# A fused attention and two-layer feed-forward kernel: attention's loads issued by ScalarE, the weight sums' stores by GpSimd, a second set of sums in the first pair

## The chip, the cores and the metric

One core of a Trainium2 chip. The metric is the device time of one execution, in microseconds. DVE is VectorE, ACT is ScalarE, POOL is GpSimd, SP is SyncE; PE is TensorE.

## The reference

Three functions in a chain, all in float32, over 4 batches of 768 tokens (3,072 in all) with 8 heads of 64.

```python
for c in range(S // 32):                      # chunks of 32 queries
    k_full = concat(mem_k, k[l_start:r_end])  # 8 memory keys; 16 to the left, 8 to the right
    a = softmax(q_c @ k_full.T / 8)
    out[chunk] = a @ v_full
x  = out as tokens x 512
xn = x / sqrt(mean(x * x) + 1e-6) * rms_g
h1 = (silu(xn @ w_gate) * (xn @ w_val)) @ w_out            # 512 -> 1536 -> 512
h  = h1 @ w_in
g  = where(h >= 1, h, where(h <= -1, 0, (h + 1)**2 / 4))
y  = g @ w_out2                                            # 512 -> 2048 -> 512
```

## The kernel before

**Arithmetic.** Every matrix product of the feed-forward layers is made of three products of high and low parts (lines 578 to 580 and 902 to 904): an operand is split into `hi`, rounded by ScalarE, and `lo`, the difference, made by DVE or GpSimd. The weights arrive as 64-bit words and are joined to float32 from the two halves of a word (`conv_c`, `join`).

**Tiles and stages.** The tokens are six tiles of 512 (TT). Tiles 0 to 3 (NS = 4) go one by one through the first layer: 12 blocks `f` of 128 features, three slots each, so 36 slots to a tile. Tiles 4 and 5 form a *pair* that is worked with seven products in place of eight (`seven`), on sums and differences of quarters of the inputs and of the weights. After it three pairs go through the second layer in the same way. Up to about 46 us the start is laid out engine by engine; tile 0 lasts to about 152 us, tiles 1 to 3 to about 269, 380 and 490 us, the first pair to about 640 us.

**What sets the order.** From tile 1 on every engine's order is the order in which the program writes its instructions. Each slot of a tile is a fixed place for background work, and `slot()` runs in it, in this order: what the slot before left in `later`, the attention step of that slot, one step of `xq` (if it has any), `conv_step`, and what stands in `after`.

**Attention beside the tiles.** A *unit* is four heads of 256 tokens; `pr` counts pairs of two units. `att_slot` with the table `plan2` spreads a pair over 11 slots: scores `s0` and `s1` in slots 0 and 3, transposes `a0`, `a1` in 2 and 5, values `v0`, `v1` in 4 and 7, normalization `r0` in 9, and transposes of the finished rows `x0`, `x1` in 10 and 12. Right after a unit's scores `att_step` loads k_in (two) and q_in of the next unit (`load_qk`, lines 391 and 392), after its values v_in (`load_v`). Line 425 is the scores, 450 the exponentials, 455 the transposes of them, 471 the values, 511 the squares, 530 the reciprocal root rs on GpSimd, 538 and 541 the scaling of x_nat, 551 its transposes, 567 their copies with rms_g (g_t), and 569 the stores of the finished x into DRAM (x_d) for tiles 2 and later.

**Sums of weights.** In tiles 1 to 3 a list of small steps (`steps`, taken by `conv_step`) prepares what the pairs need. `sum_steps` builds the first layer's sums, `w2_steps` and `pair_sums` the second layer's. A set of sums is two tiles S: DVE writes them (`sums`, lines 192 to 196), ScalarE rounds them (`hi_s`, 199), DVE takes the difference (`lo_s`, 202), and both parts are stored to DRAM (w1p_d, w1o_d, w2p_d, w2o_d; line 204). The quarters that need no sum go to DRAM as they are (`raws`, lines 239 and 243, "w1p_d<-wall"; for the second layer line 297). `load_w2` (line 270) loads the second layer's words into a ring of three tiles. The last of these steps run in the first pair, where S is the one tile `m2["late"]`.

**Preparing the pair.** In tile 3 both tiles' x come back as y from x_d (line 800), and `x_steps` makes the seven combinations from it in 12 steps, one per slot: the first is DVE's line 842, the rounding is ACT's 832, the differences are DVE's 835. `proj_in` and line 867 and 879 are the first layer's own gate and product, 593 and 595 the split of the hidden tile h into hh and hl. In the pair `seven` keeps three products per block in a ring `t` (`tmp2`; lines 922, 929, 933, 949, 954, 955).

Which queue carries what, before: SP the attention loads, x_d, the sums' stores, and all weight loads of the pairs; GpSimd the raws and the second layer's words.

Of the kernel before, what the change touches and what calls it, by code (L numbers as in the profile page):

```python
# [8 lines left out]
F32 = mybir.dt.float32  # L9
F32R = mybir.dt.float32r  # L10
BF16 = mybir.dt.bfloat16
U32 = mybir.dt.uint32
# [4 lines left out]
P = 128  # L17
# [14 lines left out]
TT = 512  # L32
# [8 lines left out]
def tile_stream_attention_moe_moe2(  # L41
# [10 lines left out]
    nc = tc.nc  # L52
    NT, DM = out.shape
    F1 = wts1.shape[0] // 3
    F2 = wts2.shape[0] // 2
    KK = DM // P
# [4 lines left out]
    pool = lambda name, bufs, **kw: ctx.enter_context(tc.tile_pool(name=name, bufs=bufs, **kw))  # L61
# [8 lines left out]
    moe1_only = ctx.enter_context(ExitStack())  # L70
    pool1 = lambda name, bufs: moe1_only.enter_context(tc.tile_pool(name=name, bufs=bufs))
    const1 = pool1("const1", 1)
    small = pool1("small", 2)
    wst = pool1("wst", 3)
    tmp = pool1("tmp", 3)
    single_only = moe1_only.enter_context(ExitStack())
# [3 lines left out]
    wall2 = poolS("wall2", 1).tile([P, 15, 2, 512], F32R, name="wall2")  # L80
    sp = poolS("sp", 3)
    sums_ = poolS("sums", 1)

    half = const.tile([P, 1], F32, name="half")

# [1 line left out]
    ident = const.tile([P, P], F32, name="ident")  # L87
    wall = wpool.tile([P, 21, 2, 512], F32R, name="wall")
    g_b = const1.tile([P, DM], F32, name="g_b")
    nhalf = const1.tile([P, 2], F32, name="nhalf")  # L90
    g_t = const1.tile([P, KK], F32, name="g_t")

    def unit(i):
        if i < 14:
# [14 lines left out]
    NS = NTT - 2  # L109
# [91 lines left out]
    def lo_s(S, k, h, dst):  # L201
        tt_(out=flat(S[k]), in0=flat(S[k]), in1=h.bitcast(F32), op=ALU.subtract)
        for n, src in enumerate((h.bitcast(F32), flat(S[k]))):
            nc.sync.dma_start(dst(n, k), src.rearrange("p (k c) -> p k c", k=2))

    def in_dst(dp):
        return lambda n, k: dp[:, 3 + 2 * k:5 + 2 * k, n]
# [6 lines left out]
    def at(n, fn):  # L214
        while len(steps) <= n:
            steps.append([])
        steps[n].append(fn)
# [4 lines left out]
    def sum_steps(i, srcs, raws, order, dst):  # L222
        n = 8 * i
        h, S = [], []

        def whole():
            if i % 2:
                h.extend(tmp.tile([P, 512], U32, tag="tu", name="wgv") for _ in range(2))
            else:
                gv = wst.tile([P, 1024], U32, tag="w64", name="wgv")  # L230
                h.extend([gv[:, :512], gv[:, 512:]])
            for x, w in zip(h, srcs):
                tt_(out=x.bitcast(F32), in0=w[:, 0], in1=w[:, 1], op=ALU.add)

        def first():
            S.extend(halves(wst.tile([P, 1024], F32, tag="w64", name="s1234")))
            sums(S, *order(h), True)

        at(n, lambda: (nc.gpsimd.dma_start(*raws[0]), whole()))
        at(n + 1, first)  # L240
        at(n + 2, lambda: sums(S, *order(h), False))
        for k, r in enumerate(raws[1:]):
            at(n + 2 + 2 * k, lambda r=r: nc.gpsimd.dma_start(*r))
        at(n + 4, lambda: hi_s(S, 0, h[0]))
        at(n + 5, lambda: hi_s(S, 1, h[1]))
        at(n + 6, lambda: lo_s(S, 0, h[0], dst))
        at(n + 7, lambda: lo_s(S, 1, h[1], dst))
# [18 lines left out]
    def load_w2(j):  # L266
        if j < 2 * F2:
            g, k = divmod(j, 4)
            w2raw[j] = wst.tile([P, 1024], U32, tag="w64", name="w64")
            nc.gpsimd.dma_start(w2raw[j], wts2[4 * g + (0, 2, 1, 3)[k]].bitcast(U32))  # L270

    W2 = 12 * F1 + 4

    def w2_steps(g):

        dp, do, u = w2p_d[g], w2o_d[g // 2], g % 2
        f32_ = {}

        part = lambda j, n: w2raw[j][:, 512 * n:512 * n + 512]

        def c(j):
            f32_[j] = g_b.bitcast(U32) if j % 4 == 3 else tmp.tile([P, 512], U32, tag="tu", name="tu")
            nc.scalar.activation(f32_[j].bitcast(F32), words(w2raw[j])[1].bitcast(F32), AF.Prelu, scale=2.0 ** -112, alpha=2.0 ** 32)

        def hi(j, n0, n1):
            nc.scalar.activation(part(j, 0)[:, n0:n1].bitcast(F32R), f32_[j].bitcast(F32)[:, n0:n1], AF.Copy)

        def lo(j, n0, n1, dsts):
            tt_(
                out=part(j, 1)[:, n0:n1].bitcast(F32),  # L290
                in0=f32_[j].bitcast(F32)[:, n0:n1],
                in1=part(j, 0)[:, n0:n1].bitcast(F32),
                op=ALU.subtract,
            )
            src = w2raw[j].bitcast(F32).rearrange("p (h c) -> p h c", h=2)
            for dst, c0, c1 in dsts:
                nc.gpsimd.dma_start(dst, src[:, :, c0:c1])

        dsts = [
            [(dp[:, 0], 0, 256), (dp[:, 1], 256, 512)],  # L300
            [(dp[:, 2], 256, 512)],
            [(do[:, 0, u], 0, 256)],
            [(do[:, 3, u], 0, 256), (do[:, 6, u], 256, 512)],
        ]
        for k in range(4):
            j, n = 4 * g + k, W2 + 28 * g + 7 * k
            n0, n1 = ((0, 512), (256, 512), (0, 256), (0, 512))[k]
            at(n, lambda j=j: c(j))
            at(n + 2, lambda j=j: join(f32_[j], w2raw[j]))
            at(n + 4, lambda j=j, n0=n0, n1=n1: hi(j, n0, n1))  # L310
            at(n + 6, lambda j=j, n0=n0, n1=n1, k=k: lo(j, n0, n1, dsts[k]))
            at(n + 13, lambda j=j: load_w2(j + 3))
        def pair_sums(a, b, n, order, dst):
            S, h = [], lambda: (f32_[a], f32_[b])

            def first():
                if m2["single"]:
                    S.extend([sp.tile([P, TT], F32, tag="s", name="s12"), sums_.tile([P, TT], F32, tag="s34", name="s34")])
                else:
                    S.extend(m2["late"][:, i] for i in range(2))  # L320
                S[:] = [x.rearrange("p (k c) -> p k c", k=2) for x in S]
                live.append(a)
                sums(S, *order(h()), True)

            at(n + 10, first)
            at(n + 11, lambda: sums(S, *order(h()), False))
            at(n + 13, lambda: hi_s(S, 0, f32_[a]))
            at(n + 14, lambda: hi_s(S, 1, f32_[b]))
            at(n + 15, lambda: lo_s(S, 0, f32_[a], dst))
            at(n + 16, lambda: (lo_s(S, 1, f32_[b], dst), live.remove(a)))  # L330

        pair_sums(4 * g, 4 * g + 1, W2 + 28 * g, rows_order, in_dst(dp))
        pair_sums(4 * g + 2, 4 * g + 3, W2 + 28 * g + 14, cols_order, out_dst(do, u))
# [44 lines left out]

    tails = []

    def load_qk(u):
        if u >= NU:
            return
        if u in (1, 2):
            kt = [hp_.tile([P, TT], F32, tag=t, name="k_in") for t in ("hh", "hl")]
            qt = sp.tile([P, TT], F32, tag="s", name="q_in")
        else:
            kt = [att.tile([P, TT], F32, tag=f"k{hp}", name="k_in") for hp in range(2)]
            qt = att.tile([P, 2 * PT], F32, tag="q", name="q_in")
        for hp in range(2):  # L390
            nc.sync.dma_start(kt[hp], k[u][:, hp * 512:hp * 512 + 512])
        nc.sync.dma_start(qt, q[u])
        qk_t[u] = (kt, qt)

    def load_v(u):
        if u >= NU:
            return
        n = 8 * (D + 1)
        if u < 4:
            if not tails:  # L400
                tails.append(xs.tile([P, 4, 2, D + 1], F32, tag="xn", name="v_tail"))
            tail = tails[0][:, u]
            nc.sync.dma_start(tail, v[u].rearrange("p (h c) -> p h c", h=2)[:, :, n - D - 1:])
            vt = [xs.tile([P, TT], F32, tag=f"x{'hl'[hp]}{u}", name="v_in") for hp in range(2)]
            m = n - D - 1
        else:
            vt = [att.tile([P, n], F32, tag=f"v{hp}", name="v_in") for hp in range(2)]
            m = n
        for hp in range(2):
            nc.sync.dma_start(vt[hp][:, :m], v[u][:, hp * n:hp * n + m])  # L410
        v_t[u] = [
            [tail[:, hp] if c == 7 and u < 4 else vt[hp][:, c * 65:c * 65 + 65] for c in range(8)]
            for hp in range(2)
        ]
# [139 lines left out]
    def part_X(pr, blk):  # L554
# [11 lines left out]
            for kk in range(KK):  # L566
                nc.scalar.activation(xn[:, kk], rows[:, kk], AF.Copy, scale=g_t[:, kk:kk + 1])
        if t >= 2:
            nc.sync.dma_start(x_d[t][:, :, c0:c0 + P], xn)

    def load_x(t):
        xn_t[t] = xs.tile([P, KK, TT], F32, tag="xn", name="xn")
# [158 lines left out]
    def att_step(pr, st):  # L731
# [8 lines left out]
        else:  # L740
            u = 2 * pr + n
            fns[st[0]](u, ps_a)
            for p in parts[st[0]]:
# [2 lines left out]
                    fn()  # L746
                else:
                    (later if p in "kp" else after).append(fn)
        if st[0] == "s":
            load_qk(2 * pr + n + 1)  # L750
        if st[0] == "v":
            load_v(2 * pr + n + 1)

    xq, after, later = [], [], []

# [39 lines left out]
    wo = {}  # L795
# [59 lines left out]
    for t in range(NS):  # L855
# [3 lines left out]
        for f in range(F1):  # L859
# [5 lines left out]
            proj_in(ps_g[0], w1[("g", f)])  # L865
            s = sp.tile([P, TT], F32, tag="s", name="s")
            nc.scalar.activation(s, ps_g[0], AF.Silu)
            slot(t, 3 * f)
            if t == NS - 1 and f == 6:
                att_only.close()  # L870
                right = ctx.enter_context(tc.tile_pool(name="right", bufs=1, side="right", reuse_waits="tile"))
                m2["y"] = right.tile([P, 2, KK, TT], F32, name="y")
                load_y(x_d[NS], x_d[NS + 1])
            if t == NS - 1 and f == 7:
                xq.extend(x_steps())
            proj_in(ps_g[1], w1[("v", f)])
            if f == F1 - 1 and t + 1 < NS:
                split_x(xn_t.pop(t + 1))
# [257 lines left out]
            m2[part] = parts[part]()  # L1136
        m2["n"] = 0

    second_pool(F1 // 2, 5, 6, "ring t wo h")
    m2["late"] = m2["pool"].tile([P, 2, TT], F32, name="s1234")  # L1140
    pair_bank.close()
    bpool = ctx.enter_context(
        tc.tile_pool(name="bpool", bufs=1, space=bass.MemoryType.PSUM, side="right", reuse_waits="tile")
# [135 lines left out]
```

## Time and profile before

| | |
|---|---|
| median of 3 runs | 1171.7 us (1169.03 to 1171.91) |
| the profiled execution | 1173.91 us |
| its span in the trace | 1172.1 us |
| mean granted TensorE clock | 0.987 of full speed |
| busy: TensorE, DVE, ScalarE, GpSimd | 97%, 70%, 53%, 10% of the span |
| moved by DMA | 281.81 MB, 240 GB/s over the span |

The span begins at the first instruction and ends with the last; times in the rows are microseconds from its start. "Busy" counts instructions in execution; issuing a DMA is shown in the rows under the issuing engine's queue (SPq, ACTq, POOLq) or engine, but is not counted. An instruction starts when its engine has come to it in program order and everything that it waits for has come: what ended its wait last stands in brackets behind it.

### The profile page before, as it was taken

What the parts mean: (1) busy time and instruction counts of PE and PEld (TensorE: products, weight loads), DVE (VectorE), ACT (ScalarE), POOL (GpSimd) and SP (SyncE); (2) the same over time, 40 slices, a digit from 0 to 9 for tenths busy, and PEclk for the clock granted to TensorE, in tenths of its full rate; (3) what the DMA queues carried; (4) which work ended last, traced back from release to release, by engine and by line L of the source; (5) the groups of instructions that cost most, each with busy time, mean ns of one, the idle gap of its engine ahead of it and who ended that gap; (6) DMA issues with size and microseconds to landing.
All of it is one profiled execution on the core that took longest, in us unless ns stands there. A gap on an engine that the chain in (4) does not pass through costs nothing.

```text
span 1172.1 us, 21039 instructions
## 1 busy us (share of the span) xinstructions
PE 1131.2 (97%) x7909; PEld 915.6 (78%) x7909; DVE 821.4 (70%) x1426; ACT 619.0 (53%) x1096; POOL 114.9 (10%) x165
## 2 busy tenths in 40 slices
PE   7889999999999999899989999999999999999998
PEld 5677787788787778788768888778887788887886
DVE  4777767677656676656647877897767887578855
ACT  4676655467665675434433734456434465444543
POOL 2500003122212123101110000000000000000000
PEclk7899999999999999999999999999999999999999
DMA  9765538798988797779998687766778666773564
GB/s 311 235 228 193 181 135 286 249 345 294 302 250 303 228 312 225 261 276 335 400 346 261 203 284 244 256 179 195 230 210 260 180 191 212 219 202 95 151 194 159
DMA packets 144212, 281.81 MB, mean 240 GB/s; under 512 B 15216, under 2 KB 65392, under 8 KB 142320
## 3 DMA queue, kind: packets, MB, share of 16 engines
q1 hardware_dynamic: 123664, 228.57, 60.9%
q0 software_dynamic: 12768, 43.52, 11.1%
q10 hardware_dynamic: 7680, 8.39, 2.0%
q8 instruction: 62, 1.02, 0.3%
q14 instruction: 38, 0.31, 0.1%
HBM read 201.26 MB, written 79.17 MB: 239 GB/s over the span
## 4 chain that ended last, share of the span: by engine, by line
PE 74%; DMA 9%; DVE 8%; ACT 5%; issue 2%; SPq 1%; POOL 1%; ACTq 0%; DVEq 0%; POOLq 0%
PE ps_y L1064 14%; PE ps_g L1064 10%; PE ps_g L578 5%; PE ps_g L580 5%; PE ps_g L579 5%; DMA w<-in_w_dram 3%; PE ps_g L902 3%; PE ps_b L902 3%; PE ps_b L904 3%; PE ps_b L903 3%; PE ps_g L904 3%; PE ps_g L903 3%; PE ps_y L578 3%; PE ps_y L579 2%; PE ps_y L580 2%
## 5 line engine op out<-in xcount | busy, mean ns | idle before, releaser
L1064 PE MATMUL ps_y<-r,wo 128*128 128x512 f32 x672 | 156.2, 390 | 0.0
L578 PE MATMUL ps_g<-xh,wall 128*128 128x512 f32 x384 | 156.1, 406 | 0.0
L580 PE MATMUL ps_g<-xh,wall 128*128 128x512 f32 x384 | 150.4, 392 | 0.0
L579 PE MATMUL ps_g<-xl,wall 128*128 128x512 f32 x384 | 150.3, 391 | 0.0
L1064 PEld LDWEIGHTS ps_y<-r,wo 128*128 128x128 f32 x672 | 125.7, 188 | 26.0
L1014 DVE TENSOR_TENSOR r<-h,r 128x512 fp32r<-128x512 f32 x167 | 112.0, 687 | 44.4 <-ACT r L1012 44.4
L965 ACT ACTIVATE t<-t,half 128x512 f32<-128x512 f32 x96 | 66.9, 720 | 128.4 <-DVE t L964 122.7
L1012 ACT ACTIVATE r<-h 128x512 fp32r<-128x512 f32 x167 | 100.7, 625 | 56.5 <-DVE r L1014 17.5
L1064 PE MATMUL ps_g<-r,wo 128*128 128x512 f32 x498 | 116.0, 390 | 0.0
L1064 PEld LDWEIGHTS ps_g<-r,wo 128*128 128x128 f32 x498 | 93.2, 188 | 19.4
L580 PEld LDWEIGHTS ps_g<-xh,wall 128*128 128x128 f32 x384 | 72.4, 188 | 15.9
L578 PEld LDWEIGHTS ps_g<-xh,wall 128*128 128x128 f32 x384 | 72.6, 189 | 15.6 <-issue 0.2
L902 PE MATMUL ps_b<-wall 128*128 128x512 f32 x202 | 79.9, 396 | 4.3 <-DVE t L933 4.0
L579 PEld LDWEIGHTS ps_g<-xl,wall 128*128 128x128 f32 x384 | 72.7, 189 | 13.5
L902 PE MATMUL ps_g<-wall 128*128 128x512 f32 x198 | 78.8, 398 | 4.3 <-DVE t L933 2.4
L904 PE MATMUL ps_b<-wall 128*128 128x512 f32 x202 | 79.2, 392 | 0.0
L903 PE MATMUL ps_b<-wall 128*128 128x512 f32 x202 | 79.2, 392 | 0.0
L579 PE MATMUL ps_y<-hl,wall 128*128 128x512 f32 x192 | 75.8, 395 | 3.0 <-DVE hl L595 3.0
L578 PE MATMUL ps_y<-hh,wall 128*128 128x512 f32 x192 | 78.1, 407 | 0.0
L903 PE MATMUL ps_g<-wall 128*128 128x512 f32 x198 | 77.3, 390 | 0.0
L904 PE MATMUL ps_g<-wall 128*128 128x512 f32 x198 | 77.2, 390 | 0.0
L580 PE MATMUL ps_y<-hh,wall 128*128 128x512 f32 x192 | 75.5, 393 | 0.0
(191 smaller groups left out, 2112.1 us busy)
## 6 DMA issues: line engine op xcount, KB each, us to landing
wo<-w2o_d SPq DMA_DIRECT2D x88, 512.0 KB, 3.6
wall<-w2p_d SPq DMA_DIRECT2D x168, 256.0 KB, 3.0
wall<-w1p_d SPq DMA_DIRECT2D x84, 256.0 KB, 5.7
w<-in_w_dram SPq DMA_DIRECT2D x36, 512.0 KB, 4.9
w<-in_w_dram POOLq DMA_DIRECT2D x32, 512.0 KB, 5.7
k_in<-in_k_dram SPq DMA_DIRECT2D x48, 256.0 KB, 4.7
wo<-w1o_d SPq DMA_DIRECT2D x21, 512.0 KB, 3.6
v_in<-in_v_dram SPq DMA_DIRECT2D x40, 260.0 KB, 4.4
```

The source lines that it names most:

```text
L578: nc.tensor.matmul(ps, wh, xh, start=start, stop=False)
L579: nc.tensor.matmul(ps, wh, xl, start=False, stop=False)
L580: nc.tensor.matmul(ps, wl, xh, start=False, stop=stop)
L902: nc.tensor.matmul(bank, wh, xh, start=st, stop=False, skip_group_check=True)
L903: nc.tensor.matmul(bank, wh, xl, start=False, stop=False, skip_group_check=True)
L904: nc.tensor.matmul(bank, wl, xh, start=False, stop=kk == 1, skip_group_check=True)
L965: nc.scalar.activation(s, s, AF.Square, scale=0.5, bias=half)
L1012: nc.scalar.activation(r[:, 0], src, AF.Copy)
L1014: tt_(out=r[:, 1], in0=src, in1=r[:, 0].bitcast(F32), op=ALU.subtract)
L1064: nc.tensor.matmul(bank[p][m], a, b, start=s0, stop=s1, skip_group_check=True)
```

## The change

Attention's loads for pairs 4 and later and the x_d stores are issued by ScalarE; the loads stand first in `after`, ahead of the exponentials or squares. The sums' stores (`lo_s`) go onto GpSimd's queue; the raws and `load_w2` go to SP. The first pair has two sets of sums and takes them in turn; the ring `t` has five tiles in place of six. `x_steps` begins with slot 24 (before it) in place of slot 22. The statistics tiles (ss, rs), nhalf and g_t are allocated last among the pools of the single tiles.

```diff
-    small = pool1("small", 2)
...
     sums_ = poolS("sums", 1)
+    small1 = poolS("small1", 1)
+    small = poolS("small", 2)
...
-    nhalf = const1.tile([P, 2], F32, name="nhalf")
-    g_t = const1.tile([P, KK], F32, name="g_t")
+    nhalf = small1.tile([P, 2], F32, name="nhalf")
+    g_t = small1.tile([P, KK], F32, name="g_t")
...
     def lo_s(S, k, h, dst):
...
-            nc.sync.dma_start(dst(n, k), src.rearrange("p (k c) -> p k c", k=2))
+            nc.gpsimd.dma_start(dst(n, k), src.rearrange("p (k c) -> p k c", k=2))
...
-        at(n, lambda: (nc.gpsimd.dma_start(*raws[0]), whole()))
+        at(n, lambda: (nc.sync.dma_start(*raws[0]), whole()))
...
-            at(n + 2 + 2 * k, lambda r=r: nc.gpsimd.dma_start(*r))
+            at(n + 2 + 2 * k, lambda r=r: nc.sync.dma_start(*r))
...
     def load_w2(j):
...
-            nc.gpsimd.dma_start(w2raw[j], wts2[4 * g + (0, 2, 1, 3)[k]].bitcast(U32))
+            nc.sync.dma_start(w2raw[j], wts2[4 * g + (0, 2, 1, 3)[k]].bitcast(U32))
...
-                    S.extend(m2["late"][:, i] for i in range(2))
+                    S.extend(m2["late"][a // 2 % 2][:, i] for i in range(2))
...
-    def load_qk(u):
+    def load_qk(u, eng=nc.sync):
...
-    def load_v(u):
+    def load_v(u, eng=nc.sync):
...
         if t >= 2:
-            nc.sync.dma_start(x_d[t][:, :, c0:c0 + P], xn)
+            nc.scalar.dma_start(x_d[t][:, :, c0:c0 + P], xn)
...
-        if st[0] == "s":
-            load_qk(2 * pr + n + 1)
-        if st[0] == "v":
-            load_v(2 * pr + n + 1)
+        if st[0] in "sv":
+            load = load_qk if st[0] == "s" else load_v
+            if pr < 4:
+                load(2 * pr + n + 1)
+            else:
+                after.insert(0, lambda: load(2 * pr + n + 1, nc.scalar))
...
+            if t == NS - 1 and f == 8:
+                xq.extend(x_steps())
             slot(t, 3 * f)
...
-            if t == NS - 1 and f == 7:
-                xq.extend(x_steps())
...
-    second_pool(F1 // 2, 5, 6, "ring t wo h")
-    m2["late"] = m2["pool"].tile([P, 2, TT], F32, name="s1234")
+    second_pool(F1 // 2, 5, 5, "ring t wo h")
+    m2["late"] = [m2["pool"].tile([P, 2, TT], F32, name=f"late{i}") for i in range(2)]
```

The line numbers of the changed kernel are one to three higher. The change moves instructions at three places that matter below. First SP's queue before, in tile 1, at a unit's scores; x_d is the store of finished rows, w1p_d the stores of sums (s_2317 their low parts, wgv the rounded ones):

```order
L569 DMA x_d_116<-x_nat 512x1x128
L204 DMA w1p_d_134<-wgv 128x2x256
L204 DMA w1p_d_134<-s_2317 128x2x256
L204 DMA w1p_d_134<-wgv 128x2x256
L204 DMA w1p_d_134<-s_2317 128x2x256
L391 DMA k_in<-in_k_dram 128x512 x2
L392 DMA q_in<-in_q_dram 128x512
L569 DMA x_d_116<-x_nat 512x1x128
```

The same place on ScalarE with the change:

```order
L594 ACTIVATE hh<-s 128x512
L568 ACTIVATE x_nat<-ps_a,g_t 128x128 x4
L570 DMA x_d_119<-x_nat 512x1x128
L392 DMA k_in<-in_k_dram 128x512 x2
L393 DMA q_in<-in_q_dram 128x512
L451 ACT_TABLE_LOAD
L451 ACTIVATE e<-e 128x512
L870 ACT_TABLE_LOAD
```

The loads stand between the copies of x_nat and the table load of the exponentials now, and the x_d stores have come along. Second, GpSimd before, in tile 2, where rs is made (w_... are the second layer's words):

```order
L270 DMA w_4495<-in_w_dram 128x1024
L297 DMA w2p_d_121<-w_4276 128x2x256 x2
L270 DMA w_4581<-in_w_dram 128x1024
L297 DMA w2p_d_121<-w_4391 128x2x256
L530 TENSOR_TENSOR rs<-ss,nhalf 128x2
L270 DMA w_4637<-in_w_dram 128x1024
L297 DMA w2o_d_128<-w_4495 128x2x256
```

and with the change:

```order
L205 DMA w2o_d_131<-s_4332 128x2x256
L205 DMA w2o_d_131<-g_b 128x2x256
L205 DMA w2o_d_131<-s_4333 128x2x256
L298 DMA w2p_d_124<-w_4273 128x2x256 x2
L298 DMA w2p_d_124<-w_4388 128x2x256
L531 TENSOR_TENSOR rs<-ss,nhalf 128x2
L205 DMA w2p_d_124<-tu 128x2x256
```

The word loads have gone; in their place the sums' stores (line 205) stand around rs. Third, VectorE before, in tile 3, where the inputs of the pair begin (line 842, y):

```order
L879 TENSOR_TENSOR s<-s,ps_g_109 128x512
L842 TENSOR_TENSOR y<-y 128x1024
L142 TENSOR_SCALAR tu<-tu 128x512
L143 SCALAR_TENSOR_TENSOR tu<-w_5619,tu 128x512
L202 TENSOR_TENSOR s_5652<-s_5652,tu 128x512
L595 TENSOR_TENSOR hl<-s,hh 128x512
L289 TENSOR_TENSOR w_5619<-tu,w_5619 128x256
L835 TENSOR_TENSOR wall<-y,wall 128x2x512
```

and with the change:

```order
L882 TENSOR_TENSOR s<-s,ps_g_112 128x512
L143 TENSOR_SCALAR tu<-tu 128x512
L144 SCALAR_TENSOR_TENSOR tu<-w_5622,tu 128x512
L203 TENSOR_TENSOR s_5655<-s_5655,tu 128x512
L596 TENSOR_TENSOR hl<-s,hh 128x512
L290 TENSOR_TENSOR w_5622<-tu,w_5622 128x256
L845 TENSOR_TENSOR y<-y 128x1024
L882 TENSOR_TENSOR s<-s,ps_g_112 128x512
```

y begins two slots later: the rest of its block's work, with the split of h (hl), comes first now, and y stands five rows further down, ahead of the next block's product.

## Rows read from the trace of the kernel before

**Rows 1.** The page, busy shares: busy us, share of the span, instructions.
```profile
PE 1131.2 (97%) x7909; PEld 915.6 (78%) x7909; DVE 821.4 (70%) x1426; ACT 619.0 (53%) x1096; POOL 114.9 (10%) x165
```

**Rows 2.** TensorE's waits: what waited <- for what; us in total, times, longest.
```profile
PE ps_s L551 <- DVE x_nat L541: 5.3, 1, 5.3
PE ps_a L425 <- DMA q_in<-in_q_dram: 4.1, 4, 2.9
PE ps_b L902 <- DVE t L933: 4.0, 1, 4.0
...
PE ps_y L579 <- DVE hl L595: 3.0, 1, 3.0
PE ps_g L902 <- DVE t L933: 2.4, 1, 2.4
...
PE ps_a L551 <- ACT x_nat L538: 1.7, 1, 1.7
```

**Rows 3.** Windows: us, busy us (instructions) of each engine, granted clock, DMA share, GB/s.
```profile
206.26:209.67 3.41, 3.41 (x70) 2.76 (x71) 2.11 (x4) 0.68 (x1) 0.00 (x0) 0.51 1.05 345
...
602.21:605.62 3.41, 3.35 (x8) 2.70 (x9) 0.72 (x3) 1.64 (x4) 0.71 (x1) 0.51 1.04 393
```

**Rows 4.** Timeline of SP's queue: start us, us, engine, line, operation.
```profile
193.13 0.65 SPq L204 DMA_DIRECT2D w1p_d<-wgv  x1
...
196.44 2.75 SPq L391 DMA_DIRECT2D k_in<-in_k_dram  x2
```

**Rows 5.** Chain that ended last, its DMA pieces: start us, us, what.
```profile
199.24 6.84 DMA q_in<-in_q_dram
...
570.45 7.34 DMA w2p_d<-s
...
591.73 8.65 DMA w2o_d<-s
```

**Rows 6.** Timeline of ScalarE: in brackets idle us before, and what ended it.
```profile
195.53 0.63 ACT L450 ACTIVATE e<-e 128x512 f32<-128x512 f32 x1 [1.76 <-DVE e L441]
```

**Rows 7.** Timeline of GpSimd (POOL).
```profile
375.84 0.55 POOL L270 DMA_DIRECT2D w<-in_w_dram  x1 [8.12 <-DMA w2p_d<-w]
```

**Rows 8.** Timeline at the start, GpSimd and VectorE.
```profile
31.49 1.45 POOL L243 DMA_DIRECT2D w1p_d<-wall  x2
...
33.71 4.24 DVE L541 SCALAR_TENSOR_TENSOR x_nat<-x_nat,rs,g_b 128x512 f32<-128x512 f32 x2 [1.82 <-POOL rs L530]
```

**Rows 9.** Timeline, TensorE and ScalarE, around the scores of a unit in tile 3.
```profile
420.89 0.86 PE L425 MATMUL ps_a<-k_in,q_in 64*32 64x64 f32 x64
...
424.83 1.28 ACT L450 ACT_TABLE_LOAD   x1
426.12 0.64 ACT L450 ACTIVATE e<-e 128x512 f32<-128x512 f32 x1
...
427.84 0.66 PE L455 MATMUL ps_a<-ident,e 128*128 128x128 f32 x4
...
431.18 0.86 PE L425 MATMUL ps_a<-k_in,q_in 64*32 64x64 f32 x64
```

**Rows 10.** Timeline of VectorE.
```profile
476.26 1.23 DVE L842 TENSOR_TENSOR y<-y 128x1024 f32<-128x1024 f32 x1 [7.14 <-DMA y<-x_d]
```

**Rows 11.** Timeline of VectorE in the first pair.
```profile
599.09 0.43 DVE L192 TENSOR_TENSOR s<-tu 128x256 f32<-128x256 f32 x1 [3.95 <-DMA w2o_d<-s]
```

**Rows 12.** DMA issues: count, KB, median us to landing; line 391: ns min/median/max.
```profile
w1p_d<-wall POOLq DMA_DIRECT2D x36, 256.0 KB, 5.0
...
q_in<-in_q_dram SPq DMA_DIRECT2D x24, 256.0 KB, 5.3
...
w1p_d<-s SPq DMA_DIRECT2D x24, 256.0 KB, 5.1
...
L391 SPq DMA_DIRECT2D k_in<-in_k_dram x48: 327/415/1574, 0.7 to 421.9; - x48
```

**Rows 13.** Windows, columns as in rows 3.
```profile
380.00:490.00 110.00, 106.91 (x958) 85.89 (x957) 72.14 (x142) 67.61 (x132) 24.94 (x37) 0.98 0.77 253
```

More of the change, by code (lines that the diff above doesn't have):

```diff
@@ L390, in load_qk @@
         for hp in range(2):
-            nc.sync.dma_start(kt[hp], k[u][:, hp * 512:hp * 512 + 512])
-        nc.sync.dma_start(qt, q[u])
+            eng.dma_start(kt[hp], k[u][:, hp * 512:hp * 512 + 512])
+        eng.dma_start(qt, q[u])
         qk_t[u] = (kt, qt)
-    def load_v(u):
+    def load_v(u, eng=nc.sync):
         if u >= NU:
@@ L409, in load_v @@
         for hp in range(2):
-            nc.sync.dma_start(vt[hp][:, :m], v[u][:, hp * n:hp * n + m])
+            eng.dma_start(vt[hp][:, :m], v[u][:, hp * n:hp * n + m])
         v_t[u] = [
```

## Prediction

> **What bounds the kernel now.** I read the page's busy shares first: TensorE is busy 97% of the span [rows 1]. No other engine can set the end by its mere amount of work, so the change is worth what TensorE's own waits are worth. The second view, TensorE's waits by what ended them, names these: 5.3 us once for the first normalized tokens, 2.9 us (the longest of four that make 4.1) for attention's q_in, 4.0 and 2.4 us for DVE's t at line 933, 3.0 us for hl, 1.7 us for x_nat behind ScalarE [rows 2]. Each wait is then followed back to the queue or buffer behind it, and that is where the parts of the change lie. The third view is the granted clock: after the waits of 2.9, 3.0 and 4.0 us TensorE runs at half clock (1.2 in place of 2.4 GHz) for 3.41 us, granted 0.51; the first and the last of these three stretches are shown [rows 3]. Work of 3.41 us at half clock takes some 1.7 us at the full one, so each of these waits costs about 1.7 us more than its own length. The waits of 1.7 and 2.4 us show no such stretch.
>
> The sum is made against the profiled execution, 1173.91 us (span 1172.1, the other 1.8 around it). It lies 2.2 us above the median of the three runs, 1171.7; I subtract the same sum from the median.
>
> **The change part by part.**
>
> *A, attention's loads on ScalarE.* At 193.13 SP begins four w1p_d stores, which stand ahead of the next unit's k_in; k_in is issued at 196.44 and takes 2.75 us for two [rows 4]; q_in is issued at 199.24 and lands 6.84 us later [rows 5], when TensorE has waited 2.9 us [rows 2]. The four stores take 3.3 us of SP and leave its queue altogether. ScalarE at this place idles 1.76 us until 195.53, waiting for DVE's e [rows 6], so it reaches the three loads before SP did, and they go about 4 us earlier. Saved: 2.9 + 1.7 = **4.6**. Bounds: 0 (the landing grows as much) and 4.6.
>
> *B, second-layer loads off POOL.* At 375.84 POOL issues a load of w for which it had waited 8.12 us [rows 7]; the rs behind it makes ScalarE's x_nat late, and TensorE waits 1.7 us for that [rows 2]. With loads on SP the rs no longer stands behind that wait. In place of them stand stores, 0.7 us each (two in 1.45 us [rows 8]), which can delay an rs by one or two of them. Saved: **1.7**, at least 0. On SP the same wait of 8.12 us holds raws, other second-layer loads and the next tile's xn. That xn is requested at f = 9 and split at f = 11, some 7 slots ahead; a slot is (431.18 - 420.89)/3 = 3.43 us [rows 9], so 24 us minus 8.12 leave 16 for the transfer: no cost.
>
> *C, preparing the pair's inputs two slots later.* DVE stands at line 842 for 7.14 us until y has landed, at 476.26 [rows 10]; hl, queued behind it, lets TensorE wait 3.0 us [rows 2]. Two slots later are 6.9 us of other work first, hl among it; about 0.3 us of the wait for y is left, which nobody feels. The twelve steps then fill slots 24 to 35 exactly. Saved: 3.0 + 1.7 = **4.7**; at least 0, if the last step is late for the pair's first product by as much.
>
> *D, two sets of sums in the first pair.* DVE's line 192 waits until the store of the single set has landed: 3.95 us at 599.09 for w2o_d [rows 11], whose landing took 8.65 us, and before that the w2p_d store of 570.45 took 7.34 us [rows 5]. The t that TensorE wants is queued behind line 192, hence its 4.0 and 2.4 us [rows 2]. With two sets a buffer comes back one set of sums later, more than 20 us after the store was issued (570.45 and 591.73 are two neighbours' stores [rows 5]). Saved: 2.4 + 4.0 + 1.7 = **8.1**; at least 0. The ring of t goes from six to five; three are taken per block, so a tile returns in the last third of the following block, after its last reader: no cost.
>
> *E, the start.* POOL's two raws at 31.49 take 1.45 us and stand ahead of rs, for which DVE's line 541 waits 1.82 us [rows 8]; TensorE's 5.3 us hang on that. They go to SP. ss is ready about 1 us before POOL gets to rs: **1.0** saved, between 0 and 1.45.
>
> *F, what is given back.* 75 attention loads and 16 x_d stores, 91 issues, go onto ScalarE. SP's median for one is 415 ns (327 to 1574) [rows 12]: 38 us, or 55 at 0.6 each, an estimate for crowded places. In 380 to 490 us ScalarE is busy 67.61 of 110 us [rows 13], so there is room in sum; the place decides. The tightest: scores at 420.89 last 0.86 and end at 421.75; ScalarE comes to the table load that now follows the three loads only at 424.83 [rows 9]. Three issues are 1.26 us; q_in lands 5.3 us after its issue [rows 12], at 431.4, and the next scores began at 431.18: 0.2 late. The exponentials, begun at 426.12, end at 426.76 and were wanted at 427.84; 1.26 later they are 0.2 late. Some three or four of the eight pairs of units have such a place: I take 0.4 each, **1.5** in all; bounds 0 and the first rival's 11.5.
>
> The 110 stores of sums add about 80 us to POOL, which loses its loads and raws for them and is busy 24.94 of 110 us [rows 13]; of what is queued there only rs has somebody waiting. Their landing is no worse: 5.0 us from POOL, 5.1 from SP for w1p_d [rows 12]. The small statistics tiles at the end of the pool only change addresses: nothing.
>
> Sum: 4.6 + 1.7 + 4.7 + 8.1 + 1.0 = 20.1 saved, 1.5 given back, 18.6 net. 1173.9 - 18.6 = 1155.3; against the median **1153**.
>
> **A rule against it.** In row terms, A's q_in took 6.84 us to land where its median is 5.3 [rows 5, 12]: 1.5 us of the delay was the transfers' own crowding, and the 4 us of issue were the rest. The Trainium skill ("DMA: Bandwidth & Descriptors", section "Issuing engines are not separate DMA queues") says that transfers started by different engines share the same 16 DMA engines, and that a second issuer saves only the time on the sequencer, usually small. Taken at its word A would save next to nothing, 4.6 us less. The trace agrees on the landings (5.0 and 5.1) but not on the small: three issues on SP there last from 196.44 to past 199.24, behind 3.3 us of stores. I keep A, and the crowding has a chance of its own as rival 2.
>
> **The rivals.**
> 1. *ScalarE is late with several loads while it converts second-layer weights (269 to 490 us).* For: the 0.2 us above. Against: it has a third of its time free. Two or three waits of 4.6 us, the price of the one that stands in the rows: 11.5 more, **1164**. Chance 0.14.
> 2. *Crowding, not issue, was what delayed q_in.* Then A's 4.6 stay: **1158**. Chance 0.08.
> 3. *The pair's sums still wait*, since the stores from POOL land later there than 20 us, or another buffer of DVE's binds: D's 8.1 stay, **1161**. Chance 0.06.
> 4. *Slower: ScalarE becomes the late issuer as a rule.* The load issued after a pair's first scores is wanted 10.3 us after they began, and there are eight such. Wanted 9.43 us after the scores' end, it lands 5.3 after the last of three issues of 1.26 in all: if ScalarE comes more than 9.43 - 5.3 - 1.26 = 2.9 us after the scores' end, TensorE waits. At 421.75 it is 3.1 [rows 9]; were it 5.8 everywhere, each would cost 2.9 + 1.7. 8 x 4.6 = 37 on top of 1153: **1190**. Against it: at 195.53 it idles [rows 6]. Chance 0.06.
> 5. *The change doesn't do what it says*: each wait is replaced by the next one just behind it, **1171**. For: the waits are short, 1 to 4 us, and any second input that late restores one. Against: they lie in five places with five causes. Chance 0.05.
>
> **How the numbers follow.** The forecast, 1150 to 1157, has 0.61. The range reaches from 1147 (the three runs spread by 2.9 us, and F may cost nothing) to 1165, through rivals 1 to 3; rivals 4 and 5 and the tails are left out. About 0.3% (3.5 us) is what a measurement of this kernel can tell from no change. Faster by more: 0.61 + 0.14 + 0.08 + 0.06 = 0.89; within it 0.05; slower 0.06.
>
> **What would show it right or wrong.** Right: TensorE's list of waits has no q_in of 2.9, no hl, no t over 1 us; no half-clock stretch after 46 us in the attention tiles and at 602; q_in issued within 3 us of the scores' end; no wait of DVE for a w2p_d or w2o_d store at line 193 (line 192 before); POOL's rs not behind a load. Wrong: new waits of TensorE for q_in or k_in issued by ScalarE between 269 and 490, exponentials late behind three issues, or a wait of the pair's first product for wall made from y.

## The result

The changed kernel is slower: 1187.2 us, median of four runs (1184.53 to 1189.6), against 1170.37 us (1168.5 to 1171.91, four runs of the kernel before). The ratio is 1.0144, 95% interval [1.0115, 1.0173], so 13.5 to 20.2 us slower. The forecast was 1153. The profiled execution took 1184.53 us, the fastest of its four; its span is 1182.7, 10.6 longer than the one before, so the trace shows some 6 us less of a loss than the medians.

The page's busy shares hardly move against [rows 1], except GpSimd's. GpSimd's busy time, unlike SP's and ScalarE's, does count its DMA issues, 184 now in place of 134:

```profile
PE 1134.9 (96%) x7909; PEld 916.4 (77%) x7909; DVE 820.1 (69%) x1426; ACT 618.4 (52%) x1096; POOL 158.2 (13%) x215
```

TensorE's waits, the view of [rows 2] (lines are one to three higher now):

```profile
PE ps_a L552 <- ACT x_nat L539: 6.9, 3, 3.9
PE ps_a L472 <- DMA v_in<-in_v_dram: 6.4, 4, 2.8
PE ps_a L456 <- ACT x_nat L568: 5.7, 3, 3.6
...
PE ps_b L905 <- ACT ps_b L924: 4.0, 2, 3.7
...
PE ps_s L426 <- DMA q_in<-in_q_dram: 1.7, 1, 1.7
PE ps_s L552 <- DVE x_nat L542: 1.5, 1, 1.5
```

hl and the t of line 933, which cost 3.0, 2.4 and 4.0 us before, are gone, and so is the single q_in wait of 2.9 us. In their place stand x_nat behind ScalarE's line 539 (1.7 before), v_in, the copies of line 568, and a PSUM bank, ps_b, that ScalarE has to clear. Seven stretches after 46 us are at half clock in place of three. The first, at 69.44, is in tile 0, behind a wait of 2.4 us for aT; the second and the last, as in [rows 3]:

```profile
178.67:182.08 3.41, 3.41 (x10) 2.67 (x9) 2.93 (x7) 1.67 (x3) 0.72 (x1) 0.50 1.05 388
...
608.75:612.16 3.41, 3.41 (x10) 2.66 (x9) 3.34 (x8) 0.00 (x0) 0.00 (x0) 0.50 1.03 406
```

Where the time went is plainest when the same matmul is looked up in both traces and its two starts are subtracted. TensorE's order did not change, so this can be done for each of its 7909 matmuls. The difference, each start counted from its own span's start, is -6.2 us by 114 us of the kernel before, +17.8 at 425 us: **23.9 us** are lost in between, in tiles 1 to 3. At hl it falls by 4.8, at the first of the two t waits by 2.5, rises by 6.4 up to and behind ps_b, falls by 5.8 at the second t wait; 10.9 is left at the end. So C and D came as forecast, the start gave more, and nearly all that was lost was lost where queues had been exchanged. Four places show how.

**ScalarE ahead of the exponentials** (timeline of its queue, where A was to save 4.6 us [rows 4 to 6]):

```profile
192.64 0.64 ACTq L570 DMA_DIRECT2D x_d<-x_nat  x1
193.39 2.93 ACTq L392 DMA_DIRECT2D k_in<-in_k_dram  x2
196.37 1.94 ACTq L393 DMA_DIRECT2D q_in<-in_q_dram  x1
198.33 1.28 ACT L451 ACT_TABLE_LOAD   x1 [5.73 <-issue]
```

x_d stands behind the copies, the two k_in take 2.93 us and q_in 1.94, and only then comes the table load, 5.73 us after ScalarE's last arithmetic. Before, SP spent this time. q_in is in time now, but the transposes of the exponentials wait for ScalarE. The exponentials are done at 200.26, 3 us before. What ends last are the next copies of line 568, which now stand behind the loads, the exponentials and a second table load; they read ps_a, the one PSUM tile that the transposes write:

```profile
202.06 1.13 ACT L568 ACTIVATE x_nat<-ps_a,g_t 128x128 f32<-128x128 f32 x4
203.25 1.12 PE L456 MATMUL ps_a<-ident,e 128*128 128x128 f32 x4 [3.56 <-ACT x_nat L568]
```

So at A's own place a wait of 3.6 us came for the one of 2.9 that went, and a half clock comes with it (202.56), as one had come with q_in's (206.26 in [rows 3]).

**GpSimd's queue ahead of rs** (its timeline in tile 3, at the second largest of TensorE's three waits for line 539):

```profile
423.60 0.72 POOL L298 DMA_DIRECT2D w2p_d<-w  x1 [5.86 <-DVE rd L496]
424.32 0.72 POOL L205 DMA_DIRECT2D w2p_d<-tu  x1
425.30 0.72 POOL L205 DMA_DIRECT2D w2p_d<-s  x1 [0.26 <-DVE tu L143]
430.70 0.73 POOL L205 DMA_DIRECT2D w2p_d<-tu  x1 [4.68 <-issue]
431.43 0.73 POOL L205 DMA_DIRECT2D w2p_d<-s  x1
432.18 0.72 POOL L531 TENSOR_TENSOR rs<-ss,nhalf 128x2 f32<-128x2 f32 x1
```

Three stores are issued one after another, the fourth stands 4.68 us for no wait that the profile names, and rs comes after it. ScalarE, 4.19 us idle, and then TensorE (2.7 us) wait for rs:

```profile
432.94 1.33 ACT L539 ACTIVATE x_nat<-x_nat,rs 128x512 f32<-128x512 f32 x2 [4.19 <-POOL rs L531]
```

**SP running ahead.** SP has neither attention's loads nor the sums' stores to wait for now, and sends the first layer's raws as fast as it can (SP's timeline, tile 1):

```profile
159.47 2.73 SPq L244 DMA_DIRECT2D w1p_d<-wall  x2
162.24 1.33 SPq L240 DMA_DIRECT2D w1o_d<-wall  x1
```

A k_in among them takes 9.60 us to land (chain that ended last; 4.7 was its median before):

```profile
161.72 9.60 DMA k_in<-in_k_dram
```

and ScalarE's v_in goes out at 171.22 only, when a raw that it has nothing to do with has landed, at 171.14 (ScalarE's timeline; in brackets its idle time before the next arithmetic):

```profile
171.22 1.69 ACTq L411 DMA_DIRECT2D v_in<-in_v_dram  x2
172.96 0.42 ACT L512 ACTIVATE sq<-x_nat 128x256 f32<-128x256 f32 x1 [4.78 <-DMA w1o_d<-wall]
```

TensorE then waits for v_in at the values:

```profile
176.16 0.35 PE L472 MATMUL ps_a<-v_in,aT 64*32 64x65 f32 x16 [1.97 <-DMA v_in<-in_v_dram]
```

**The second layer's words in the pair** (SP's timeline). The words stand among the loads of wall now:

```profile
592.76 0.33 SPq L271 DMA_DIRECT2D w<-in_w_dram  x1
595.24 8.58 SPq L810 DMA_DIRECT2D wall<-w1p_d  x7
```

The word issued at 592.76 is there 12.8 us later; ScalarE, in order, can't clear ps_b before, and TensorE stands 3.7 us:

```profile
605.58 0.66 ACT L284 ACTIVATE tu<-w 128x512 f32<-128x512 f32 x1 [7.59 <-DMA w<-in_w_dram]
```

Two of the gains, for comparison (DVE's timeline): rs at the start [rows 8] is waited for 0.81 us in place of 1.82, and y [rows 10] 0.90 in place of 7.14:

```profile
490.24 1.23 DVE L845 TENSOR_TENSOR y<-y 128x1024 f32<-128x1024 f32 x1 [0.90 <-DMA y<-x_d]
```

### The profile page after: what moved, and what is told of

It reads as the page before. It is cut to its first block, busy times and chain, and to the rows that moved or that the text cites. A ratio compares the mean times of both kernels' runs of the same rounds, so it can differ in the third digit from the quotient of the medians.

```text
span 1182.7 us, 21049 instructions
## 1 busy us (share of the span) xinstructions
PE 1134.9 (96%) x7909; PEld 916.4 (77%) x7909; DVE 820.1 (69%) x1426; ACT 618.4 (52%) x1096; POOL 158.2 (13%) x215
## 4 chain that ended last, share of the span: by engine, by line
PE 69%; DMA 10%; DVE 8%; ACT 7%; issue 3%; ACTq 1%; POOL 1%; SPq 1%; DVEq 0%; POOLq 0%
PE ps_y L1067 14%; PE ps_g L1067 10%; PE ps_g L579 5%; PE ps_g L580 4%; PE ps_g L581 4%; DMA w<-in_w_dram 4%; PE ps_g L905 3%; PE ps_b L905 3%; PE ps_b L907 3%; PE ps_b L906 3%; PE ps_g L906 3%; PE ps_g L907 3%; PE ps_y L579 2%; PE ps_y L580 2%; PE ps_y L581 2%
## 5 line engine op out<-in xcount | busy, mean ns | idle before, releaser
L1067 PEld LDWEIGHTS ps_g<-r,wo 128*128 128x128 f32 x498 | 93.2, 188 | 19.3 <-DVE r L1017 0.2
```

The source lines that it names most:

```text
L1067: nc.tensor.matmul(bank[p][m], a, b, start=s0, stop=s1, skip_group_check=True)
```

## The experiments

All kernels below keep what is not a queue: two sets of sums, the later start of x_steps, the order of the pools. They differ in who issues what. Times are against the kernel before, measured beside each on the same chip (medians 1167.8 to 1170.3 us).

### Undoing the exchanges, one and both

The changed kernel's two exchanges are A (k_in, q_in, v_in and x_d on ScalarE) and the swap (the sums' stores on GpSimd; raws and words on SP). Theory 1 put the loss on the swap, theory 2 on ScalarE.

```diff
queues_back, loads_on_sp (A undone):
-  after.insert(0, lambda: load(2 * pr + n + 1, nc.scalar))
+  load(2 * pr + n + 1)
-  nc.scalar.dma_start(x_d...)
+  nc.sync.dma_start(x_d...)
queues_back, stores_back (swap undone):
-  nc.gpsimd.dma_start(dst(n, k), ...)   # lo_s
+  nc.sync.dma_start(dst(n, k), ...)
-  nc.sync.dma_start(*raws...) / (w2raw[j], ...)
+  nc.gpsimd.dma_start(*raws...) / (w2raw[j], ...)
```

queues_back: 

> All queues as before; kept are the two sets of sums, the later start of x_steps and the statistics tiles at the end. Both theories expect the gains C (4.7) and D (8.1) alone: 1170.4 - 12.8 = about 1158 us, without the waits of TensorE for hl and for t at line 933.

stores_back: 

> Attention's loads and x_d stay on ScalarE; sums' stores are on SP again, raws and second-layer words on GpSimd. Theory 1 (the swap of the stores' and raws' queues lost the time: SP, rid of its waits, sends raws in bursts that crowd attention's loads): 1153 to 1158 us, v_in and k_in land within 5 us. Theory 2 (issuing on ScalarE lost it, by long issues ahead of the exponentials): 1172 to 1182 us, TensorE still waits for the copies and exponentials of ScalarE.

loads_on_sp: 

> The swap stays (sums' stores on GpSimd, raws and words on SP), attention's loads and x_d are on SP again. Theory 1: 1175 us or more, since the raws now stand ahead of the loads in SP's queue and crowd them. Theory 2: 1150 to 1157 us.

| kernel | A | swap | ratio to before | 95% interval |
|---|---|---|---|---|
| queues_back | no | no | 0.9933 | [0.9907, 0.9958] |
| stores_back | yes | no | 0.9994 | [0.9975, 1.0013] |
| loads_on_sp | no | yes | 1.0005 | [0.9986, 1.0024] |
| changed kernel | yes | yes | 1.0144 | [1.0115, 1.0173] |

C and D alone gain 0.67%, 7.8 us of the 12.8 forecast. Part of the rest is a new wait of the pair for loads of wall, 2.3 us, with a half clock (580.2); the q_in wait is still there:

```profile
PE ps_a L426 <- DMA q_in<-in_q_dram: 4.8, 2, 3.0
...
PE ps_y L902 <- DMA wall<-w1p_d: 2.3, 1, 2.3
```

Each exchange costs about 7 to 8 us, both together 25. Neither theory alone is right, and the two do harm each other: about 9 us of the loss are in neither column alone. v_in accounts for about as much: neither stores_back nor loads_on_sp has a wait for it in TensorE's list, the changed kernel has 6.4 us and two half-clock stretches with them (178.67 and 260.59), 9.8 us in all by the prediction's 1.7 for a stretch.

### Why rs is late: GpSimd holds three stores at a time

loads_on_sp leaves the swap by itself. Its TensorE waits:

```profile
PE ps_a L552 <- ACT x_nat L539: 9.2, 3, 4.8
PE ps_b L902 <- ACT ps_b L921: 3.5, 1, 3.5
```

```diff
second_sums_sp, against loads_on_sp: the second layer's sums are stored from SP
-  def lo_s(S, k, h, dst):
+  def lo_s(S, k, h, dst, eng=nc.sync):
...
-  nc.gpsimd.dma_start(dst(n, k), ...)
+  eng.dma_start(dst(n, k), ...)
...   # the first layer's sums stay on GpSimd
-  lo_s(S, 0, h[0], dst)
+  lo_s(S, 0, h[0], dst, nc.gpsimd)
```

> loads_on_sp, but the second layer's sums are stored from SP; its words stay on SP too, so GpSimd has only the second layer's raws then. If rs was late because it stood behind stores that wait until one of three earlier ones has landed, TensorE's 9.2 us for x_nat of line 539 and the half clocks behind them go: 10 to 13 us below loads_on_sp, with the wait of 3.5 us for ps_b kept. If rs is late for another reason: within 3 us of loads_on_sp.

0.9918 [0.9889, 0.9947]: 10 us below loads_on_sp, as expected. The wait for line 539 is a quarter, the one for ps_b stays in sum:

```profile
PE ps_b L902 <- ACT ps_b L921: 3.6, 2, 1.9
...
PE ps_a L552 <- ACT x_nat L539: 2.3, 1, 2.3
```

The second layer's stores on GpSimd make line 539 late in two ways, and this edit takes away both. In loads_on_sp 3.9 of the 9.2 us, and 2.7 of 6.9 in the changed kernel, stand behind an rs that comes 5 us after its sums of squares. The largest wait of each, 4.8 and 3.9 us, does not: there rs starts 0.1 us after them. DVE, and with it the sums of squares, had waited for a store to land before it could write the next sums, since tiles 1 to 3 have one set. In the changed kernel GpSimd issued that store at 374.88, 4.7 us after its data were ready, and it landed at 382.82 (timelines of DVE and GpSimd; DVE waited 0.35 us there before):

```profile
382.84 0.42 DVE L194 TENSOR_TENSOR s<-tu 128x256 f32<-128x256 f32 x1 [6.11 <-DMA w2o_d<-s]
...
387.55 1.22 POOL L531 TENSOR_TENSOR rs<-ss,nhalf 128x2 f32<-128x2 f32 x1 [0.92 <-DVE ss L525]
```

```diff
raws_pool, against the changed kernel: the first layer's raws on GpSimd too
-  nc.sync.dma_start(*raws[0])
+  nc.gpsimd.dma_start(*raws[0])
...   # and so the other raws, raws[1:]
```

> As the changed kernel, but the first layer's raws are issued by GpSimd beside the sums' stores. If the burst of raws on SP made v_in late (ScalarE's issue waits for a raw's landing, TensorE 6.4 us for v_in): these waits go, and the kernel is 8 to 12 us faster than the changed one, so 5 to 9 us slower than before. Rival, v_in is late through ScalarE itself: TensorE's wait for v_in stays, 16 us or more slower than before.

1.0212 [1.0174, 1.0251]. The expectation is half met: no wait for v_in is left in TensorE's list, so the raws on SP had a part in making v_in late. It takes v_in on ScalarE as well: loads_on_sp, with both on SP, has no wait for it either, and w2_pool below, with v_in and raws as in the changed kernel, has 7.4 us. The time went the other way, 8 us above the changed kernel's ratio, since rs is later than ever; 15.5 of these 19.3 us stand behind an rs that starts 4.9 to 6.6 us after its sums of squares:

```profile
PE ps_a L552 <- ACT x_nat L539: 19.3, 5, 6.6
```

With the landings that the trace records, the nameless waits of GpSimd ahead of a store have one rule. Each time three of these 256 KB stores are in flight, and the fourth is issued 0.31 us after the oldest of the three has landed. So it is for all 37 such waits over 1 us in raws_pool, for the 15 in loads_on_sp, the 15 in the changed kernel (the 4.68 us at 430.70 above is one) and the 13 up to 310 us in the kernel before, where no rs was late behind them. A landing on this queue took 4.6 to 5.3 us in the median, by kernel. In kernels where words are loaded on this queue too, two to four transfers were in flight at some of the waits, words among them; what counts there was not followed up.

### What of the swap is good

```diff
first_layer_swap, against queues_back: only in sum_steps (the first layer)
-  lo_s ... nc.sync,   raws ... nc.gpsimd
+  lo_s ... nc.gpsimd, raws ... nc.sync
```

> queues_back with the stores of the first layer's sums on GpSimd and its raws on SP; the second layer's queues and the attention loads as in the kernel before. If the swap helps in the first layer (the q_in wait of 3.0 + 1.7 us and about 3 us at the start go) and harms only through the second layer (rs behind the stores, words behind SP's loads of wall): 6 to 8 us below queues_back, 13 to 15 us below the kernel before. Rival, the swap harms everywhere: about the time of the kernel before, as loads_on_sp.

0.9887 [0.9855, 0.9919], 1155.95 us: 13.4 below the kernel before, as expected. Below queues_back it is some 5 us, where 6 to 8 were expected, and the two intervals just overlap. The stores of w1p_d no longer stand ahead of k_in on SP, no single q_in wait is over 1.8 us, and rs costs 3.3 us:

```profile
PE ps_a L426 <- DMA q_in<-in_q_dram: 3.7, 3, 1.8
PE ps_a L552 <- ACT x_nat L539: 3.3, 2, 1.6
```

```diff
w2_pool, against the changed kernel: words on GpSimd
-  nc.sync.dma_start(w2raw[j], ...)
+  nc.gpsimd.dma_start(w2raw[j], ...)
```

> As the changed kernel, but the second layer's words are loaded by GpSimd again. If those loads were late behind SP's loads of wall in the first pair, ScalarE's wait of 7.6 us for w there goes, and with it 3.7 + 1.5 us of TensorE: about 1182 us. If the words' queue does not matter: 1187 us, with the same wait of TensorE for ps_b.

A miss: 1.0146 [1.0105, 1.0187], no better. The words are late on this queue too: TensorE waits for ps_b 6.8 us,

```profile
PE ps_b L905 <- ACT ps_b L924: 6.8, 1, 6.8
```

and the timelines of GpSimd and ScalarE show why: the word's issue stands behind a store of sums that has waited 6.75 us, it needs 9.8 us to come, and ScalarE stands 7.44 us for it. The profile names ScalarE for the 6.75 us, but the stored sums had been rounded at 571.69; three stores were in flight, and the oldest landed 0.33 us before this issue:

```profile
582.91 0.72 POOL L205 DMA_DIRECT2D w2p_d<-tu  x1 [6.75 <-ACT t L952]
...
584.55 0.58 POOL L271 DMA_DIRECT2D w<-in_w_dram  x1
...
594.32 0.66 ACT L284 ACTIVATE tu<-w 128x512 f32<-128x512 f32 x1 [7.44 <-DMA w<-in_w_dram]
```

### What of A costs

```diff
loads_behind_exp, against stores_back
-  after.insert(0, lambda: load(..., nc.scalar))
+  after.append(lambda: load(..., nc.scalar))
```

> As stores_back, but ScalarE's loads stand behind the exponentials (or squares) of the slot in place of ahead. Theory: what stores_back lost (6.1 us against queues_back) is the time of the issues ahead of the exponentials; then TensorE's waits for ScalarE's copies (4.9 us) and exponentials (1.7 us) go, and in their place q_in is late again by some 3 us, since ScalarE reaches the loads at the time at which SP reached them: 3 to 7 us below the kernel before. Rival: the load on ScalarE's queue as such costs, wherever it stands: the waits for the copies stay, no gain on the kernel before.

A miss: 1.0019 [0.9998, 1.004]. The wait for the copies is half that of stores_back (below), the one for the exponentials is not smaller, and v_in, behind the squares now, is late:

```profile
PE ps_a L472 <- DMA v_in<-in_v_dram: 4.8, 2, 3.1
...
PE ps_a L456 <- ACT e L451: 3.0, 2, 2.8
PE ps_a L456 <- ACT x_nat L568: 2.4, 1, 2.4
```

So it is not only the place before the exponentials. Then every part of A by itself, and every pair, on top of queues_back:

| on ScalarE | ratio | 95% interval |
|---|---|---|
| none (queues_back) | 0.9933 | [0.9907, 0.9958] |
| k_in, q_in (qk_only) | 0.9930 | [0.9904, 0.9956] |
| v_in (v_only) | 0.9905 | [0.9881, 0.9930] |
| x_d (xd_only) | 0.9897 | [0.9870, 0.9925] |
| k_in, q_in, v_in (qk_v) | 0.9929 | [0.9903, 0.9955] |
| k_in, q_in, x_d (qk_xd) | 0.9968 | [0.9949, 0.9986] |
| v_in, x_d (v_xd) | 0.9888 | [0.9861, 0.9916] |
| all (stores_back) | 0.9994 | [0.9975, 1.0013] |

qk_only: 

> queues_back with k_in and q_in alone on ScalarE (45 issues). If stores_back's 6.1 us are the three issues ahead of the exponentials: the whole of it, 5 to 6 us slower than queues_back (some 1 us below the kernel before), with TensorE's waits for the transposes behind ScalarE. If every issue costs alike, half of it: 3 us.

v_only: 

> queues_back with v_in alone on ScalarE (30 issues). First view: within 1 us of queues_back, 6 to 8 us below the kernel before. If every issue costs alike: 2 us slower than queues_back.

xd_only: 

> queues_back with the stores x_d alone on ScalarE (16 issues). Both views: within 1 us of queues_back, 6 to 8 us below the kernel before.

qk_v: 

> queues_back with k_in, q_in and v_in on ScalarE, x_d on SP (75 issues). If the loads and v_in's place behind them are what adds up: about the time of the kernel before, as stores_back. If it takes x_d: 5 to 8 us below the kernel before.

qk_xd: 

> queues_back with k_in, q_in and x_d on ScalarE, v_in on SP (61 issues). If x_d ahead of three loads is what makes the exponentials late: about the time of the kernel before, as stores_back. If it takes v_in: 5 to 8 us below it.

v_xd: 

> queues_back with v_in and x_d on ScalarE, k_in and q_in on SP (46 issues). Neither stands ahead of the exponentials: as v_only and xd_only, 9 to 12 us below the kernel before. If v_in and x_d are the pair that costs: 3 us below it or less.

No single part costs anything, against both views for qk_only. The pair that does is k_in and q_in with x_d: qk_xd lies 8 us above xd_only, and their intervals don't meet. Above queues_back and qk_only it lies 4 us, and there the intervals overlap. In ScalarE's timeline x_d and the three loads follow one another there, and the table load of the exponentials comes 4.51 us after the last arithmetic:

```profile
190.21 0.59 ACTq L570 DMA_DIRECT2D x_d<-x_nat  x1
191.39 1.81 ACTq L392 DMA_DIRECT2D k_in<-in_k_dram  x2
193.30 1.37 ACTq L393 DMA_DIRECT2D q_in<-in_q_dram  x1
194.69 1.28 ACT L451 ACT_TABLE_LOAD   x1 [4.51 <-PE ps_g L581]
```

Without x_d ahead (qk_v) it comes after 2.79 us; the two k_in take 1.05 us there and q_in 0.47:

```profile
193.49 1.28 ACT L451 ACT_TABLE_LOAD   x1 [2.79 <-issue]
```

TensorE's waits bear this out in part only. For the copies and the exponentials together they are 4.6 us in qk_xd and 2.5 in qk_v, but 7.5 in the trace of qk_only (3.3 for the copies, and the line below), which is of the slowest of its five runs:

```profile
PE ps_a L456 <- ACT e L451: 4.2, 2, 3.9
```

So that the pair costs is measured; how it does is read from one place and not shown. stores_back, with all three, has these waits of TensorE:

```profile
PE ps_a L456 <- ACT x_nat L568: 4.9, 3, 2.6
...
PE ps_a L426 <- DMA q_in<-in_q_dram: 3.0, 2, 2.1
...
PE ps_a L456 <- ACT e L451: 1.7, 2, 1.6
```

Why v_in adds some 3 us more to qk_xd (the intervals touch) is not settled.

### The parts that gained, together

```diff
swap1_xd, against first_layer_swap:      x_d on nc.scalar
swap1_v_xd, against swap1_xd:            v_in on nc.scalar
```

swap1_xd: 

> first_layer_swap (the swap of queues in the first layer alone) with x_d on ScalarE. If x_d costs nothing there: as first_layer_swap, 12 to 15 us below the kernel before. If ScalarE's queue is as dear as SP's was: 2 us less of a gain.

swap1_v_xd: 

> The parts that gained, together: the swap of queues in the first layer alone, v_in and x_d on ScalarE, k_in and q_in on SP, and what queues_back keeps. If the gains of first_layer_swap (13 us) and of v_xd over queues_back (5 us) add: 17 to 19 us below the kernel before. If both only free SP at the same place (the q_in wait): 13 to 15 us below it.

swap1_xd is 0.9872 [0.9844, 0.9901], as expected and equal to first_layer_swap within the intervals; swap1_v_xd 0.9915 [0.9884, 0.9946], less of a gain than either expectation. The gains don't add. That each frees SP's queue ahead of the same q_in is one reason that was not tested; the trace shows another. swap1_v_xd has v_in on ScalarE and raws on SP, as the changed kernel, and TensorE waits for v_in again, which swap1_xd does not:

```profile
PE ps_a L472 <- DMA v_in<-in_v_dram: 5.4, 4, 1.9
```

swap1_xd, 15 us below the kernel before and 32 below the changed one, is the lowest that was run; first_layer_swap and v_xd are equal to it within the intervals.

## Why the prediction was wrong

- **A** was right in its place and wrong in its price. The q_in wait of 2.9 us and the half clock behind it went, in the changed kernel as in stores_back, but at the same place the copies on ScalarE now cost TensorE 3.6 and 2.6 us, and a half clock too. And the prediction took the issues at 415 ns, the median of [rows 12], where its own [rows 4] showed 1.4 us each in that place; in the changed kernel they took 1.5 and 1.9 us there. The issue time was moved to an engine that has exponentials and copies waiting behind it. The rule of the Trainium skill ("DMA: Bandwidth & Descriptors", section "Issuing engines are not separate DMA queues") that a second issuer saves issue time alone came nearer: k_in and q_in on ScalarE change the time by nothing (0.9930 against 0.9933). But the issues are not small beside the transfers here (1.5 and 1.9 us beside landings of 4.2 and 5.0 in the median), and the engine they move to loses what the other saves.
- **F**, the term that failed. 1.5 us were given back in it, 0.4 each at three or four places where the exponentials would be late; the copies behind them, which hold ps_a, were not in it. A and F together were to gain 3.1 us; stores_back loses 7 with them (0.9994 against 0.9933).
- **B** had the wrong sign. "Stores, 0.7 us each, which can delay an rs by one or two of them" counted the issue only. A store behind three others waits until one has landed, up to 5.8 us in the changed kernel: the rs and the sums behind such stores cost TensorE 6.9 us there, 9.2 in loads_on_sp, and rs 1.7 before.
- **What had no term at all**: that SP, without its waits, sends raws in bursts, which made v_in on ScalarE late, 6.4 us of TensorE that went when the raws left SP; and the words in the pair, on SP among loads of wall, 3.7 us and a half clock. The prediction had looked at the words' wait on SP in tiles 1 to 3 only.
- **C** measured 4.8 (4.7 forecast), **D** 8.3 (8.1) in the aligned traces. **E** was forecast at 1.0; in the seven kernels with the first layer's raws on SP the first normalized tokens come 2.0 to 4.5 us earlier than before (4.4 in the changed one), in the ten with raws on GpSimd between 1.2 earlier and 1.1 later. Why they gain more than the wait for rs was not followed up.
- **Rival 4** named the right engine and sign at 0.06, with another mechanism: ScalarE late with k_in and q_in. q_in was in time. Late were the copies behind the loads and the exponentials, and v_in. The threshold that it gave, 2.9 us after the scores' end, was never what decided. **Rival 1**, 0.14, had ScalarE late between 269 and 490 us; of the 5.7 us for the copies 2.1 lie there, and the largest wait is at 203.

## What to carry to other kernels

A DMA moved from one queue to another is not taken off the path; price its issue by the rows of the crowded place, not by the median, and list what computes behind it on its new engine. A queue that loses its waits sends what is left in it earlier, and that lands among the transfers that matter. Keep short arithmetic that others wait for, as rs here, and stores that a buffer waits for, off an engine that issues more than three stores in a row, as GpSimd did here.

## What the hardware showed that was not expected

GpSimd issued at most three 128 x 2 x 256 float32 stores before it stopped, and went on 0.31 us after the oldest had landed, in every one of the waits counted above. An issue took 0.33 us for the word at 592.76 and 0.9 to 1.9 us in the crowded places (qk_xd, the changed kernel), and what ScalarE had to compute behind it began only after it. ScalarE's loads and SP's raws held each other up in another way too: the two issues of v_in at 171.22 and 172.58 came 0.08 and 0.10 us after a raw of w1p_d and one of w1o_d had landed (4.78 us of ScalarE idle at 172.96), though they share no data. The compiled program names a DMA counter beside TensorE as what the first of them waits for, and in the trace that w1p_d raw, issued by SP at 160.78, is the last to have used this counter:

```
L411 DMA v_in<-in_v_dram 128x520 [waits DMAHW2_49,PE_49]
```

In the changed kernel six of the 30 issues of v_in on ScalarE came within 0.1 us of such a landing of SP's raws, in raws_pool none.
